# Two loads, one store and the first microseconds of a fused attention and feed-forward kernel, rearranged

## The chip, the cores and the metric

One Trainium2 chip, one core of it. The metric is the device time of one execution in microseconds (us). Before the change the median of three runs is 107.88 us (107.62 to 108.11). One further execution was profiled; it took 107.41 us, and the span that its profile covers is 105.6 us.

The engines are named as the profile names them: PE (matrix multiply, with PEld for its weight loads), DVE (vector), ACT (scalar), POOL (GpSimd) and SP (the queue that issues most DMAs).

## The reference, cut to what matters

```python
def phi(x):                                   # r = 8, so phi(x) has 64 features
    a = einsum('rd,bhsd->bhsr', S1, x); b = einsum('rd,bhsd->bhsr', S2, x)
    return einsum('bhsi,bhsj->bhsij', a, b).reshape(..., 64)
q_p, k_p = phi(q), phi(k)                     # batch 4, heads 4, sequence 1088, head size 32
kv  = einsum('bhsf,bhsd->bhfd', k_p, v);      z = sum(k_p, axis=2)
num = einsum('bhsf,bhfd->bhsd', q_p, kv);     den = einsum('bhsf,bhf->bhs', q_p, z) + 1e-6
x   = (num / den) -> 4352 tokens of 128       # heads side by side
h   = x @ w_in                                # 128 -> 2048
out = (h - tanh(h)) @ w_out                   # 2048 -> 128, float32
```

The kernel uses that `h @ w_out` is linear: it computes `x @ (w_in @ w_out)` once per token with a folded 128 x 128 matrix (kept as a high and a low bf16 half, `whi` and `wlo`), and subtracts `tanh(h) @ w_out`, for which the tanh is taken of `-h`.

## The kernel before, in words

The program is a list of operations. Each has an engine, an estimated cost, the cells that it reads and writes, and a function that issues its instructions. The order of the operations on every engine is written out as a table of numbers, `ORDER` (lines 37 to 76); each engine runs its list strictly in that order and waits on semaphores where an operand comes from another engine. A planner (`schedule`, lines 141 to 230) goes through the same list with estimated durations. It decides only one thing in the instructions: where PE gets dummy matmuls on a zero tile `wz` (the "fill", lines 187 to 201) while it would otherwise be idle before the first layer begins.

Loads are issued by SP. A load may not be issued before all but the last 2.4 MB asked for have landed (`gated`, line 419), so some loads wait in SP's queue, and everything behind them in the queue waits with them.

Batch 0 goes through a path of its own before the main phase. The keys are loaded and turned (L574), projected (L583), turned back (L591). POOL and DVE form the 64 key products of each token (`wk`, L630). PE multiplies them with the values `vx` (L643, `values_first`); ACT copies the sums (`kvs`, L649), PE folds the four strips (L652), and ACT copies the result twice, masked, into a block-diagonal `kvb` (L656). The queries run beside it: projection (L752), `qab` (L760), denominators (L779 to L788), products `qp` (L662), PE transposes (L677), ACT copies `qpB`, the numerators (L694), and the copy to `xT` (L700), which is what the first layer reads. ACT also casts parts of `w_in` to bf16 (L844), POOL the rest and all of `w_out` (L848); PE turns `w_in` (L858) and multiplies it with `w_out` to get the folded matrix (L870, "wfold").

The main phase has ten windows of tokens: 256, 256, seven of 512, 256. For every window PE does the first layer (L913), ACT the tanh (L917), PE the second layer with `w_out` as weights (L926) and the folded product (L898), all adding into one PSUM bank; DVE turns that bank into `osb` (L932), and four DMAs per window and batch store it (L939), with runs of 128 bytes. Batches 1 to 3 are attended to in between, on a separate path with its own lines.

The values of batch 0 are loaded by four DMAs (L480): each fills 32 partitions of `vx`, with four runs (heads) of 1152 or 896 bytes in each partition. `S1` and `S2` are loaded as `s_raw` with 8 rows each (L439).

Of the kernel before, what the change touches and what calls it, by code (L numbers as in the profile page):

```python
# [8 lines left out]
ALU = mybir.AluOpType  # L9
# [4 lines left out]
R = 8  # L14
# [16 lines left out]
COLD = 6800  # L31
CHUNK = 256
# [20 lines left out]
    ),  # L53
    "scalar": (
# [4 lines left out]
    ),  # L59
    "vector": (  # L60
# [5 lines left out]
    ),  # L66
    "gpsimd": (
        "24 16 2 3 4 19 5 25 6 20 7 17 18 79 80 81 110 106 22 23 107 21 109 108 111 150 152 241 242 247 251 363 365 364 370 374 "
        "506 508 507 517 513 "
    ),  # L70
    "sync": (
# [22 lines left out]
class Program:  # L94
# [46 lines left out]
    def schedule(self):  # L141
# [21 lines left out]
        while left:  # L163
# [20 lines left out]
            if e == "tensor":  # L184
                if filling and o in self.fill_stops:
                    filling = False
                if filling and fills_from in order["vector"]:
                    free[e] = max(free[e], fills_from.at + fills_from.cost + 200, 1050)
                    while True:
# [3 lines left out]
                        if free[e] + long + 60 > o.at:  # L193
                            break
# [149 lines left out]
def bass_polysketch_attn__then__act_tanh_shrink_kernel(nc, q, k, v, S1, S2, moe_w_in, moe_w_out, out):  # L344
# [26 lines left out]
    e4 = sb("e4", [4, 4, 4, 8])  # L371
    hmask = sb("hmask", [128, 2])
    pmask = sb("pmask", [128, 2])
    mask = sb("mask", [128, H, R])
# [31 lines left out]
    tt = sb("tt", [128, UNITS, UNIT], BF16)  # L406
    osb = [sb(f"osb{i}", [128, 512]) for i in range(2)]
# [38 lines left out]
    def load_rows(dst, src, name, b, cuts, prios, first=0):  # L446
        i = b % 2
        for x, (lo, hi) in enumerate(cuts):
            hi = min(hi, S)
            size = 512 * (hi - lo)  # L450
            o = P.op("sync", size / (340 if b else 290), lambda e, lo=lo, hi=hi: e.dma_start(
                out=dst[i][:, lo:hi], in_=src[b].rearrange("h (j c) d -> (h j) (c d)", j=32)[:, lo:hi]),
                w=cells(name + "raw", i, lo, hi), sem=f"{name}{i}{x + first}", prio=prios[x], name=f"load {name}{b}{x + first}",
                after=gated(size))
            o.lag = 1500 if b == 1 else 300
            asked.append((o, size))
# [18 lines left out]
    def load_v(b, prio):  # L475
        i = b % 2
        src = v[b].rearrange("h (j c) d -> j h c d", j=32)
        for g in range(4):
# [3 lines left out]
                in_=src[:, :, 9 * g:9 * g + n, :].rearrange("j h t d -> j h (t d)")), True, 190 if b == 0 else 240)  # L482
# [19 lines left out]
    def constants():  # L502
# [7 lines left out]
        P.op("gpsimd", 240, lambda e: e.memset(e4[:, :, :, :], 0.0), w=[("e4",)], prio=-999)  # L510
        P.op("gpsimd", 400, select(e4[:, :, :, :], [[0, 4], [-1, 4], [0, 8]], 0), r=[("e4",)], w=[("e4",)], prio=-999)
# [6 lines left out]
        P.op("vector", 110, lambda e: e.memset(pmask[:, :], 0.0), w=[("pmask",)], prio=-998)  # L518
        for h in range(2):
            P.op("vector", 110, lambda e, h=h: e.memset(pmask[64 * h:64 * h + 64, h:h + 1], 1.0),  # L520
                 w=[("pmask",)], prio=-998)
# [11 lines left out]
    def sketch():  # L533
        def put(e):
            for h in range(H):
                ins = e.matmul(ps[32 * h:32 * h + 32, 5, 0:32], s_raw[:, :],
                               ident[0:16, None, 0:16].to_broadcast([16, 2, 16]),
                               start=True, stop=True, tile_position=(0, 32 * h))
            return ins

        P.op("tensor", 100, put, r=[("s_raw",), ("ident",)], w=[bank[5]], prio=-3000, mode="32x32", name="psk", ni=16)
# [6 lines left out]
    def folding():  # L548
        P.op("tensor", 60, lambda e: e.matmul(
            ps[:, 6, 0:32], e4[:, :, :, :].rearrange("p a b c -> p (a b c)"), e4[:, 0, :, :].rearrange("p b c -> p (b c)"),  # L550
# [515 lines left out]
```

## Time and profile before

| what | value |
|---|---|
| median of three runs | 107.88 us |
| the profiled execution | 107.41 us, span 105.6 us |
| busy over the span | PE 97.0 us, ACT 78.5, DVE 60.4, POOL 35.9 |
| values of batch 0, issue of their last load to landing | 4.70 to 9.23 us |
| first multiplication with the values (L643) | 9.93 us |
| first matmul of the first layer (L913) | 16.25 us |
| folded product (L870) | 19.34 us |
| last turn into `osb` (L932), last store issued | 102.06 us, 102.96 us |

Times inside the profile count from the start of the span. A group line gives engine, line, operation and tiles, then busy time and the mean of one, then the idle time ahead and what ended it. A line of the timeline gives start, length, engine, line and operation. The chain follows the last instruction back through what released it.

### The profile page before, as it was taken

How to read it: one execution, taken by the hardware profiler on the slowest of the kernel's cores; microseconds unless marked ns; L12 is line 12 of the kernel's file. 1: busy time of each engine (PE TensorE's matmuls, PEld its weight loads, DVE VectorE, ACT ScalarE, POOL GpSimd, SP SyncE). 2: the span in 40 equal slices, each digit the busy share in tenths (PEclk: the TensorE clock that was granted, in tenths of full speed). 3: DMA queues.
4: the chain of work that ended last, by engine and by line, in shares of the span. 5: the costliest groups of instructions: out<-in, count | busy, mean ns of one | idle time of the engine just before them, and what ended most of it. 6: DMA issues, size and time to landing. Idle time of an engine off the chain costs nothing.

```text
span 105.6 us, 2945 instructions
## 1 busy us (share of the span) xinstructions
PE 97.0 (92%) x1243; PEld 50.2 (48%) x1254; DVE 60.4 (57%) x128; ACT 78.5 (74%) x107; POOL 35.9 (34%) x45
## 2 busy tenths in 40 slices
PE   6899899999999969989899999999999999999960
PEld 2557556774576433423644343544444434345540
DVE  2378966899899999198389546892550020200210
ACT  3340588746768836769899796989969999899930
POOL 5637058710946700884900059176000000000000
PEclk9999999999999999999999999999999999999998
DMA  2999999603841503799202300035013222015263
GB/s 46 288 218 346 321 313 243 239 20 72 261 120 19 151 20 77 189 228 253 73 0 33 51 6 0 6 53 87 0 22 50 46 43 44 0 31 91 36 94 55
DMA packets 26509, 11.21 MB, mean 106 GB/s; under 512 B 19072, under 2 KB 24320, under 8 KB 26496
## 3 DMA queue, kind: packets, MB, share of 16 engines
q1 hardware_dynamic: 25920, 10.95, 42.9%
q8 instruction: 10, 0.16, 0.6%
q10 hardware_dynamic: 576, 0.07, 0.4%
q14 instruction: 3, 0.02, 0.1%
HBM read 8.78 MB, written 2.23 MB: 104 GB/s over the span
## 4 chain that ended last, share of the span: by engine, by line
PE 58%; DMA 12%; DVE 10%; ACT 5%; SPq 4%; POOL 4%; issue 3%; POOLq 0%; DVEq 0%
PE ps L926 21%; PE ps L913 21%; DMA w_out_f<-in_moe_w_out_dram 5%; ACT tt L917 5%; PE ps L821 4%; DMA vx<-in_v_dram 4%; PE ps L898 4%; DMA out_dram<-osb 3%; DVE qpT L804 3%; POOL w_out L848 2%; DVE qp L798 2%; DVE osb L932 2%; SPq L480 2%; PE ps L752 1%; DVE qab L760 1%
## 5 line engine op out<-in xcount | busy, mean ns | idle before, releaser
L917 ACT ACTIVATE tt<-ps 128x1024 bf16<-128x1024 f32 (+1 forms) x70 | 66.9, 998 | 10.9 <-PE ps L913 10.2
L913 PE MATMUL ps<-xT,w_in 128*128 128x512 bf16 (+1 forms) x151 | 40.4, 346 | 1.3 <-issue 0.6
L926 PE MATMUL ps<-tt,w_out 128*128 128x512 bf16 (+1 forms) x158 | 39.7, 347 | 0.2 <-issue 0.2
L630 POOL TENSOR_TENSOR wk<-kab 128x768 f32<-128x768 f32 (+2 forms) x11 | 15.7, 1424 | 22.7 <-DVE kab L591 22.2
L913 PEld LDWEIGHTS ps<-xT,w_in 128*128 128x128 bf16 x160 | 14.0, 97 | 17.5 <-ACT tt L917 5.5
L926 PEld LDWEIGHTS ps<-tt,w_out 128*128 128x128 bf16 x160 | 15.3, 99 | 13.2 <-issue 1.3
L932 DVE STREAM_TRANSPOSE osb<-ps 128x512 f32<-128x512 f32 (+1 forms) x10 | 6.4, 636 | 24.1 <-PE ps L926 22.9
L798 POOL TENSOR_TENSOR qp<-qa,qab 128x768 f32<-128x768 f32 x6 | 11.2, 1867 | 7.3 <-DVE qa L788 7.1
L804 DVE STREAM_TRANSPOSE qpT<-qp 128x768 f32<-128x768 f32 x9 | 8.4, 961 | 4.1 <-POOL qp L798 4.0
L760 DVE STREAM_TRANSPOSE qab<-ps 128x576 f32<-128x576 f32 (+2 forms) x10 | 6.0, 638 | 2.5 <-PE ps L752 2.5
L740 DVE STREAM_TRANSPOSE qT<-qraw 128x576 f32<-128x576 f32 (+2 forms) x9 | 5.8, 653 | 0.0
L504 PE MATMUL ps<-wz 128*128 128x512 bf16 x9 | 4.6, 581 | 1.0 <-DVE hmask L514 1.0
L821 PE MATMUL ps<-qpT,kvw 32*32 32x288 f32 (+1 forms) x192 | 4.6, 398 | 0.8 <-DVE qpT L804 0.8
L570 DVE STREAM_TRANSPOSE kT<-kraw 128x576 f32<-128x576 f32 x6 | 4.4, 746 | 0.0
L831 ACT CAST xT<-ps 128x256 bf16<-128x256 f32 x6 | 2.1, 380 | 2.8 <-PE ps L821 2.8
L898 PE MATMUL ps<-xT,whi 128*128 128x512 bf16 (+1 forms) x10 | 3.5, 353 | 0.7 <-DVE osb L932 0.4
L798 DVE TENSOR_TENSOR qp<-qa,qab 128x768 f32<-128x768 f32 x3 | 4.0, 1346 | 0.1
L848 POOL CAST w_out<-w_out_f 128x512 bf16<-128x512 f32 x4 | 2.4, 611 | 4.5 <-DMA w_out_f<-in_moe_w_out_dram 4.1
L591 DVE STREAM_TRANSPOSE kab<-ps 128x576 f32<-128x576 f32 (+2 forms) x5 | 3.2, 656 | 1.1 <-PE ps L583 1.1
L821 PEld LDWEIGHTS ps<-qpT,kvw 32*32 32x32 f32 x192 | 2.5, 103 | 2.8 <-DVE qpT L804 1.3
L712 PEld LDWEIGHTS ps<-wk,vx 128*32 128x32 f32 x216 | 3.2, 110 | 1.2 <-issue 1.2
L712 PE MATMUL ps<-wk,vx 128*32 128x64 f32 x216 | 3.6, 220 | 0.0
(90 smaller groups left out, 90.1 us busy)
## 6 DMA issues: line engine op xcount, KB each, us to landing
vx<-in_v_dram SPq DMA_DIRECT2D x12, 144.0 KB, 3.6
qraw<-in_q_dram SPq DMA_DIRECT2D x4, 288.0 KB, 4.6
w_in_f<-in_moe_w_in_dram SPq DMA_DIRECT2D x4, 256.0 KB, 4.8
w_out_f<-in_moe_w_out_dram SPq DMA_DIRECT2D x4, 256.0 KB, 5.9
out_dram<-osb SPq DMA_DIRECT2D x16, 64.0 KB, 2.0
kraw<-in_k_dram SPq DMA_DIRECT2D x3, 288.0 KB, 4.2
kraw<-in_k_dram SPq DMA_DIRECT2D x3, 256.0 KB, 4.1
qraw<-in_q_dram SPq DMA_DIRECT2D x3, 256.0 KB, 3.1
```

Source lines behind the costliest of these rows:

```text
L630: P.op(eng, dve(cols) if eng == "vector" else pool2(cols), lambda e, t0=t0, t1=t1, ap=ap, m=m, ka0=ka0: e.tensor_tensor(out=wk[:, t0:t1, : ...
L712: ins = e.matmul(ps[32 * h:32 * h + 32, vb, 0:64], vx[i][:, h, t, :], wk[:, t, h, :, :], start=(t == 0), stop=(t == NT - 1), tile_position ...
L740: P.op("vector", dve(hi - lo), lambda e: e.transpose(out=qT[i][:, lo:hi], in_=qraw[i][:, lo:hi]), r=cells("qraw", i, lo, hi), w=cells("qT" ...
L760: P.op("vector", dve(2 * n), lambda e, h=h: e.transpose(out=qab[:, t0:t1, h:h + 2, :].rearrange("p t h x -> p h t x"), in_=ps[:, qb + h:qb ...
L798: P.op(eng, dve(cols) if eng == "vector" else pool2(cols), lambda e, p0=p0, p1=p1, w=w: e.tensor_tensor(out=qp[:, p0:p1, :, :, :].rearrang ...
L804: P.op("vector", dve(cols), lambda e, p0=p0, p1=p1: e.transpose(out=qpT[:, p0:p1, :, :, :].rearrange("p t h y j -> p (t h y j)"), in_=qp[: ...
L821: ins = e.matmul(ps[32 * h:32 * h + 32, nb[g], 0:32 * n], kvw[i][32 * g:32 * g + 32, y, 32 * h:32 * h + 32], qpT[32 * g:32 * g + 32, t0:t0 ...
L898: P.op("tensor", pe(n), lambda e, x=x: e.matmul(acc[:, 0:n], x[:, :], xT[:, f0:f0 + n], start=f0 > 0 and x is whi, stop=not f0 and x is wl ...
L913: P.op("tensor", pe(n), lambda e, jb=jb + y, y=y, hb=hb: e.matmul(hb[:, n * y:n * y + n], w_in[:, 128 * jb:128 * jb + 128], xT[:, f0:f0 + ...
L917: P.op("scalar", act(q * n), lambda e, un=un, hb=hb, q=q: e.activation(out=tt[:, un, 0:q * n], in_=hb[:, 0:q * n], func=AF.Tanh, scale=-1. ...
L926: P.op("tensor", pe(n), lambda e, jb=jb, un=un, y=y: e.matmul(acc[:, 0:n], w_out[:, jb, :], tt[:, un, n * y:n * y + n], start=(not f0 and ...
L932: P.op("vector", dve(n), lambda e: e.transpose(out=osb[u][:, 0:n], in_=acc[:, 0:n]), r=[ka], w=[("osb", u)], prio=slot0, name=f"osb{w}")
```

## The change

Four parts, and a new written-out order for all engines.

1. The dummies before 5 us may run up to 120 ns past the planned start of an operation that has just become ready; the others still have to end 60 ns ahead of it.
2. The sketch: `s2p` (L552) becomes four column tiles of the same PE pass as `psk` (L536). The matmul that made the head mask (L549) goes, with its `e4` constant; the mask is now made on DVE by four small reductions of the identity. `kvb` is cleared once on POOL and then written by two plain ACT copies of 64 partitions, instead of two masked copies of 128; `pmask` goes.
3. The values of batch 0: four loads of 96 partitions, one for each head, and one of 32 partitions for the rest. The two loads of the first 512 columns of the queries become one.
4. The last 256 tokens: their `tanh` tiles and `xT` are used as weights and `w_out`, `whi`, `wlo` as the moving operand, 128 tokens at a time, in banks 6 and 7. The result has tokens in partitions, so a DVE copy and an ACT copy take the place of the turn, and two DMAs with runs of 512 bytes, one on SP and one on ACT, that of the four with runs of 128 bytes.

```diff
-                        if free[e] + long + 60 > o.at:
+                        if free[e] + long > o.at + (120 if o.at < EARLY and o.at - o.ready < 1 else -60):
...
-        src = v[b].rearrange("h (j c) d -> j h c d", j=32)
-        for g in range(4):
+        src = v[b].rearrange("h (j c) d -> j h (c d)", j=32)
+        for x in range(0 if b else 4):
+            rows = src[:, x, 0:KG]
+            rows = bass.AP(tensor=rows.tensor, offset=rows.offset, ap=[[KG, 3], *rows.ap])
+            o = load("sync", 128 * 32 * 27, ("vx", i), f"v{i}", prio, lambda e, x=x, rows=rows: e.dma_start(
+                out=vx[i][0:96, x, :, :].rearrange("p t d -> p (t d)"), in_=rows), True, 300)
+            o.lag = 300
+        for g in range(0 if b else 3, 4):
...
+        for g in range(4):
+            P.op("vector", 110, lambda e, g=g: e.tensor_reduce(
+                out=mask[32 * g:32 * g + 32, :], in_=ident[32 * g:32 * g + 32, 32 * g:32 * g + 32].rearrange("p (h i) -> p h i", i=R),
+                axis=AX.X, op=ALU.add), r=[("ident",)], w=[("mask",)], prio=-989, name=f"mask{g}")
+        P.op("gpsimd", 240, lambda e: e.memset(kvb[:, :, :, :], 0.0), w=[("kvb", 0), ("kvb", 1)], prio=-976)
...
             for h in range(H):
+                ins = e.matmul(ps[32 * h:32 * h + 32, 6, 64:96], e16[:, :, :].rearrange("p a b -> p (a b)")[:, 32 * h:32 * h + 32],
+                               s_raw[:, :], start=True, stop=True, tile_position=(0, 32 * h))
...
-            scaled(kvb[:, :, y, :], ps[:, vb, 0:128].rearrange("p (x y d) -> p x y d", x=2, y=2)[:, :, y, :], pmask[:, y:y + 1], 64,
-                   [bank[vb], ("pmask",)], [("kvb", y)], T["kvb"], f"kvb{y}")
+            P.op("scalar", act(64), lambda e, y=y: e.copy(
+                kvb[64 * y:64 * y + 64, :, y, :], ps[64 * y:64 * y + 64, vb, 0:128].rearrange("p (x y d) -> p x y d", x=2, y=2)[:, :, y, :]),
+                r=[bank[vb]], w=[("kvb", y)], prio=T["kvb"], name=f"kvb{y}")
...
+                    for dst, _, at in halves:
+                        ins = e.matmul(dst, tt[:, un, n * y + at:n * y + at + 128], w_out[:, jb, :], start=False, stop=jb == NJB - 1)
...
+            for y, (eng, queue) in enumerate((("vector", "sync"), ("scalar", "scalar"))):
+                P.op(eng, act(128) if y else dve(128), lambda e, y=y: (e.copy if y else e.tensor_copy)(
+                    olast[:, y, :], halves[y][0]), r=[bank[6 + y]], w=[("olast", y)], prio=slot0, name=f"osb{w}")
+                c = (f0 - (B - 1) * S) // 32 + 4 * y
+                P.op(queue, 65536 / 250, lambda e, c=c, y=y: e.dma_start(
+                    out=ob[B - 1, :, c:c + 4, :].rearrange("j c e -> c j e"), in_=olast[:, y, :]),
+                    r=[("olast", y)], sem=f"outlast{y}", prio=slot0, name=f"out{w}")
...
-    load_rows(qraw, q, "q", 0, q_cuts(0)[:2], (-948, -947))
+    load_rows(qraw, q, "q", 0, ((0, 512),), (-948,))
```

The new order, in names. SP before: three key loads, two query loads, four value loads, `w_in` 0, 3, 1, 2, `w_out` 2 (which waits for the values), a query load, `w_out` 1, 0, 3. SP after: three key loads, values of head 0, the query load, values of heads 1, 2, 3 and the rest, a query load, `w_in` 1, 0, `w_out` 1 (which waits for the values), `w_in` 2, 3, `w_out` 0, 3, 2. ACT before, from the first sums on: `kvs`, cast of `w_in` 0, `kvb` twice, `qpB` twice, cast of `w_in` 1, the first `w_inT`. ACT after: casts of `w_in` 1 and 0, `kvs`, `kvb` twice, `qpB` twice, the first `w_inT`. POOL after casts `w_in` 3 and 2 ahead of all of `w_out`; before, it began with `w_out` 2. On PE the first part of the product with the values (L643) now stands ahead of the query projection (L752), and the folded product of the last window ahead of that of the window before it.

More of the change, by code (lines that the diff above doesn't have):

```diff
@@ L31 @@
 COLD = 6800
+EARLY = 5000
 CHUNK = 256
@@ L535, in put @@
             for h in range(H):
-                ins = e.matmul(ps[32 * h:32 * h + 32, 5, 0:32], s_raw[:, :],
-                               ident[0:16, None, 0:16].to_broadcast([16, 2, 16]),
-                               start=True, stop=True, tile_position=(0, 32 * h))
+                e.matmul(ps[32 * h:32 * h + 32, 5, 0:32], s_raw[:, :],
+                         ident[0:16, None, 0:16].to_broadcast([16, 2, 16]),
+                         start=True, stop=True, tile_position=(0, 32 * h))
+            for h in range(H):
+                ins = e.matmul(ps[32 * h:32 * h + 32, 6, 64:96], e16[:, :, :].rearrange("p a b -> p (a b)")[:, 32 * h:32 * h + 32],
+                               s_raw[:, :], start=True, stop=True, tile_position=(0, 32 * h))
             return ins
-        P.op("tensor", 100, put, r=[("s_raw",), ("ident",)], w=[bank[5]], prio=-3000, mode="32x32", name="psk", ni=16)
+        P.op("tensor", 170, put, r=[("s_raw",), ("ident",), ("e16",)], w=[bank[5], bank[6]], prio=-3000, mode="32x32", name="psk", ni=32)
         for h in range(2):
@@ L548, in folding @@
     def folding():
[L549 to L556 removed]
         for h in range(H):
[L558 removed]
+            scaled(s2blk[:, h, :], ps[:, 6, 64:96], mask[:, h:h + 1], 32, [bank[6], ("mask",)], [("s2blk", h)], -850, f"s2blk{h}")
     KCUT = ((0, 576), (576, NT * 128))
@@ L894, in layers, with both @@
         xs = [("x", b, c // 4, c % 4) for b, lo, m, _ in parts(f0, n) for c in range(lo // 32, (lo + m) // 32)]
+        last = f0 + n == NTOK
+        halves = [(ps[:, 6 + y, 0:128], f0 + 128 * y, 128 * y) for y in range(2)]
         def lin():
             for x, nm in ((whi, "whi"), (wlo, "wlo")):
-                P.op("tensor", pe(n), lambda e, x=x: e.matmul(
-                    acc[:, 0:n], x[:, :], xT[:, f0:f0 + n], start=f0 > 0 and x is whi, stop=not f0 and x is wlo),
-                    r=[(nm,)] + xs, w=[ka], prio=slot0 + LAG - 0.5, name=f"lin{w}")
+                if last:
+                    def both(e, x=x):
+                        for dst, f, _ in halves:
+                            ins = e.matmul(dst, xT[:, f:f + 128], x[:, :], start=x is whi, stop=False)
+                        return ins
+                    P.op("tensor", pe(n), both, r=[(nm,)] + xs, w=[bank[6], bank[7]], prio=slot0 + LAG - 0.5, name=f"lin{w}", ni=4)
+                else:
+                    P.op("tensor", pe(n), lambda e, x=x: e.matmul(
+                        acc[:, 0:n], x[:, :], xT[:, f0:f0 + n], start=f0 > 0 and x is whi, stop=not f0 and x is wlo),
+                        r=[(nm,)] + xs, w=[ka], prio=slot0 + LAG - 0.5, name=f"lin{w}")
         where = []
@@ L938, in layers @@
             for eb in range(4):
-                P.op("scalar" if last and eb % 2 else "sync", 128 * m / 250, lambda e, b=b, c=c, mc=mc, eb=eb, at=at: e.dma_start(
+                P.op("sync", 128 * m / 250, lambda e, b=b, c=c, mc=mc, eb=eb, at=at: e.dma_start(
                     out=ob[b, :, c:c + mc, 32 * eb:32 * eb + 32],
                     in_=osb[u][32 * eb:32 * eb + 32, at:at + 32 * mc].rearrange("p (c x) -> p c x", x=32)),
-                    r=[("osb", u)], sem=f"out{u}s" if last and eb % 2 else f"out{u}", prio=slot0, name=f"out{w}")
+                    r=[("osb", u)], sem=f"out{u}", prio=slot0, name=f"out{w}")
     windows = [(0, 256, (2, 2, 4, 4, 4)), (256, 256, (4, 4, 4, 4))]
```

47 lines of the change are left out of this document (20 added, 27 removed), and 52 rows, old and new, of the table ORDER.

## The prediction

> **What bounds the kernel now.** I first read the busy time by stretch: one before the first matmul of the first layer, one to the end of PE's work, and the tail.
>
> ```profile
> 0.00:16.20 16.20, 14.35 (x226) 8.38 (x227) 10.25 (x38) 7.50 (x23) 7.59 (x24) 1.00 0.91 256
> 16.20:102.00 85.80, 82.64 (x1021) 41.81 (x1029) 49.75 (x90) 71.03 (x84) 28.34 (x21) 1.00 0.35 79
> 102.00:105.60 3.60, 0.00 (x0) 0.00 (x0) 0.45 (x1) 0.00 (x0) 0.00 (x0) 0.88 0.48 73
> ```
>
> The second number after the stretch is PE's busy time: 82.64 of 85.80 us from 16.2 to 102. PE bounds the main phase (going through the starts of its bf16 matmuls I find only 4.9 us of gaps there, the largest 0.96). So only three things set the end: when the first layer begins (16.25), PE's work, and the 3.6 us behind it. Whatever moves that begin moves the end. So next the chain that ended last, then the timeline of what comes ahead of 16.25.
>
> ```profile
> 4.70 4.53 DMA vx<-in_v_dram
> 9.25 4.83 DMA w_out_f<-in_moe_w_out_dram
> ...
> 19.34 1.07 PE ps L870 x16
> ...
> 100.86 1.11 PE ps L926 x10
> 102.06 0.45 DVE osb L932
> ```
>
> ```profile
> 9.93 1.23 PE L643 MATMUL ps<-wk,vx 128*32 128x64 f32 x72
> 11.21 0.27 ACT L649 COPY kvs<-ps 128x128 f32<-128x128 f32 x1 [3.06 <-PE ps L643]
> 11.37 0.62 ACT L844 CAST w_in<-w_in_f 128x512 bf16<-128x512 f32 x1
> 13.43 0.44 PE L694 MATMUL ps<-qpB,kvb 128*64 128x128 f32 x4
> 15.86 0.27 ACT L700 CAST xT<-ps 128x128 bf16<-128x128 f32 x1
> 16.25 0.49 PE L913 MATMUL ps<-xT,w_in 128*128 128x256 bf16 x3
> 102.54 0.89 ACTq L939 DMA_DIRECT2D out_dram<-osb  x2
> ```
>
> The values land at 9.23 (4.70 + 4.53), PE takes them at 9.93, and from `kvs` (11.21) to the first layer it is 5.04 us of ACT and PE in turn. Last, the DMA issues.
>
> ```profile
> vx<-in_v_dram SPq DMA_DIRECT2D x12, 144.0 KB, 3.6
> w_in_f<-in_moe_w_in_dram SPq DMA_DIRECT2D x4, 256.0 KB, 4.8
> s_raw<-in_S_dram ACTq DMA_DIRECT2D x2, 1.0 KB
> ```
>
> The reader is to see that `s_raw` alone has no time to landing. In the trace every DMA with an outer count of 128 or 32 posts 16 updates on its semaphore; the two of `s_raw`, with 8 rows, post 18 together, that is 8 and one each. A DMA is thus shared out along its outermost count, and eight rows use eight of the sixteen engines.
>
> **The values over 96 partitions.** The new source begins with a count of 3 (`[KG, 3]`), the destination with 96. Sharing along both outermost counts leaves 3 engines. The trace shows 16 and 8, not 3, so the cost is bounded by the two ends.
>
> With 3 engines: each load has 96 runs of 1152 bytes, the four 384, so 128 on each of the three. The packet records give 51 ns for such a packet (median). 128 x 51 ns = 6.53 us. In the same three rings lie the query load (8 packets of 2048 bytes at 84 ns, 0.67) and the 32-partition load (8 at 41 ns, 0.33). The keys leave them free at about 4.1 (their last packets start between 3.9 and 4.8). 4.1 + 6.53 + 0.67 + 0.33 = 11.6; the last of these packets came 0.9 ahead of the landing before, most engines' 0.6, so the values land at about 12.3, 3.1 later than 9.23. I take this end, because it is the only reading in which the `s_raw` row and the new count obey the same thing.
>
> With 16 engines: 24 packets each at 51 ns, 1.2 us, and the landing comes at about 7.9, 1.3 earlier.
>
> [...]
>
> **What is queued behind it.** On the three rings wait the query load behind the values (8 x 93 ns) and `w_in` 1 and 0 (16 x 84 ns): 11.6 + 2.1 = 13.7, landing at 14.4. ACT now casts `w_in` 1 and 0 (0.62 each) ahead of `kvs`; these were behind it. So `kvs` begins at 14.4 + 0.62 = 15.0. PE has the values at 12.3 and needs 1.23 for the sums and 0.50 for the query projection (L752), which stands behind the first of them: 14.0, no later. From `kvs` to the first layer 5.04 become about 4.3: one cast (0.62) is gone from between and the `kvb` copies are 0.2 instead of 0.3 (L555 copies 128x32 in 0.18). First layer at 19.3: **+3.1**. The query chain (projection to numerators 3.9 us) arrives at 12.6 + 3.9 = 16.5, and with the ACT work behind it at 19 as well.
>
> SP issues `w_in` 2, 3 and `w_out` 0, 3, 2 only after `w_out` 1 has seen the values, so from 12.7 on; before, all of `w_in` was issued by 7.0. They land at 15.9 to 19.2. POOL casts `w_in` 3 and 2 by 17.9, ahead of PE's third turn (needed near 18.5), and ends `w_out` at 20.9. PE reaches the folded product at about 21, so it hides; without that cover each late cast costs 0.62. PE's gaps between 16.2 and 20 (0.6 us, half of it waiting for L870 and its casts) shrink: **-0.3**.
>
> **The sketch, the masks, the dummies.** `s2p` (0.63 at 5.04, ahead of L583 at 5.60) goes; four more tiles behind `psk` cost at most its 0.33. The key chain gains about 0.35. Four DVE reductions (0.19, row L610) for three memsets (0.06) lie in DVE's 2.23 us of waiting for the keys; POOL's identity comes at 2.5 instead of 1.84, and the masks end at 3.6 against the keys at 3.96. The clearing of `kvb` is 0.2 on POOL, early. Dummies cost 0.12 once at most. If they bring the full clock sooner, L583, L599 and L607 lose about half of their 1.21 + 0.53 + 0.58 (a 512-column dummy still takes 0.61 at 7.89 and 0.39 at 11.09): up to 0.7. All of that ends in a wait for the values: 0 here, a gain only if they land early. Merged query load: 0.
>
> **The last window.** Two matmuls of 128 columns, each with its own weights, for one of 256: L870 does sixteen in 0.93 start to start, 58 ns each, against 109 for one of L926's 256-column ones: 18 x (116 - 109) = **+0.13**. Its folded product no longer waits for `osb` of the window before: **-0.2** of the two gaps there (0.19 and 0.18). Then the store. Before, from PE's end 102.06 to the last landing at 104.60: 2.54. After: copy 0.29 (L874, 128x128 from PSUM), 0.05, issue to first packet 0.84 (99.57 to 100.41), the packets, and 0.17 to land. The outermost counts are 4 and 128, so by the same reading both DMAs share four engines: 2 x 32 packets of 512 bytes at 27 ns = 1.73. Sum 3.08, **+0.54**. On 16 engines the packets take 0.43: 1.78, -0.76.
>
> **The sum.** 3.1 - 0.3 + 0.13 - 0.2 + 0.54 = +3.3. Against the profiled execution's own time (107.41: span 105.6 and 1.8 around it) 110.7. The median of the runs is 0.47 higher; on its scale 107.88 + 3.3, so I say 111.1. The kvs chain is the least sure: 109.6 to 112.6 for this case.
>
> **The rivals.** (1) *Faster: the loads are spread over all engines.* [...] Then the values land at 7.9 and other things set `kvs`: the key products, which gain the 0.35, and the two casts, whose `w_in` lands near 10.1. First layer 0.7 earlier; the last window 0.13 - 0.2 - 0.76 = -0.83. 107.88 - 1.5 = 106.4. It decides from a landing before about 9. (2) *Slower still:* PE now stands idle from about 9.4 to 12.3, and the clock falls back. The trace shows no such fall ahead of 104.7, so its price is that of the cold rows: L599 takes 0.53 at 7.43 and 0.38 at 26.67, 1.4 times; on L643, L652 and L694 (1.23 + 0.49 + 0.44) that is +0.8: 111.9. (3) *It does nothing:* the late values meet slack that I don't see, or the loads are spread and the store is not (-0.7 + 0.47): 107.7.
>
> **Chances.** Forecast 0.60; (2) 0.12; (1) 0.23; (3) 0.05. Three runs lie within 0.25% of their median, so 0.5% is about what can be told from no change. Slower 0.72, same 0.05, faster 0.23. The range goes from 106.2, in the first rival, to 112.6.
>
> **What would show it.** Right: no time to landing for the 108 KB value loads, as for `s_raw`; L643 not before 12; `kvs` behind two casts at about 15; L913 at 19; the last packets 1.7 us long behind two issues on SP and ACT. Wrong: L643 before 9.9, which would say that the sharing does not follow the outermost count; or a late landing with L913 still near 16, which would say that ACT's order has slack.

## The result, and the profile after

The changed kernel takes **114.44 us** (median of four runs, 113.82 to 115.31), the kernel before, run beside it, 107.75 (106.87 to 108.11). The ratio is **1.064, 95% interval [1.054, 1.074]**: slower, as forecast, but by 6.7 us and not by 3.2, and outside the range, whose upper end was 112.6. The profiled execution took 114.75 us, with a span of 112.9. In the table of runs further on, executions more than 1.5% above the fastest of their kernel are left out of the ratios, but not of the medians.

The busy time by stretch of the changed kernel comes first: the same three stretches as before, namely to the first matmul of the first layer, to the end of PE's work, and the tail. The columns are the stretch, its length, and the busy time of PE, PEld, DVE, ACT and POOL, then the granted clock, the DMA share and GB/s.

```profile
0.00:22.60 22.60, 15.85 (x234) 9.49 (x235) 10.53 (x39) 7.26 (x22) 8.15 (x26) 0.77 0.67 194
22.60:108.20 85.60, 83.87 (x1050) 42.52 (x1047) 50.55 (x90) 70.78 (x84) 27.40 (x19) 1.00 0.36 76
108.20:112.90 4.70, 0.01 (x1) 0.00 (x0) 0.29 (x1) 0.27 (x1) 0.00 (x0) 0.91 0.37 69
```

The main phase is as long as it was (85.60 against 85.80). The first stretch grew from 16.2 to 22.6, the tail from 3.6 to 4.7. Next, the chain of work that ended last, from the first value load on and in its last pieces (start, length, what):

```profile
2.33 0.90 SPq L482
...
6.02 7.35 DMA vx<-in_v_dram
...
13.41 0.65 PE ps L645 x16
...
107.10 1.13 PE ps L943 x20
...
108.25 0.29 DVE olast L957
```

Behind SP's issues of the keys the chain comes to the value loads and stays on them until 13.37; before, it left them at 9.23. The timeline of the changed kernel says what follows them (start, busy time, engine, line, operation; in brackets the idle time before it and what ended it):

```profile
13.41 0.65 PE L645 MATMUL ps<-wk,vx 128*32 128x64 f32 x16 [4.24 <-DMA vx<-in_v_dram]
14.80 1.32 ACT L847 CAST w_in<-w_in_f 128x512 bf16<-128x512 f32 x2 [7.49 <-DMA w_in_f<-in_moe_w_in_dram]
15.21 1.72 PE L645 MATMUL ps<-wk,vx 128*32 128x64 f32 x56
16.99 0.27 ACT L651 COPY kvs<-ps 128x128 f32<-128x128 f32 x1 [0.87 <-PE ps L645]
20.01 1.36 POOL L847 CAST w_in<-w_in_f 128x512 bf16<-128x512 f32 x2 [10.46 <-DMA w_in_f<-in_moe_w_in_dram]
22.46 2.11 POOL L851 CAST w_out<-w_out_f 128x512 bf16<-128x512 f32 x3
22.61 0.60 PE L927 MATMUL ps<-xT,w_in 128*128 128x256 bf16 x4
25.12 1.06 PE L873 MATMUL ps<-w_out,w_inT 128*128 128x128 bf16 x16
```

PE stands idle for 4.24 us before the values come. The product with them (L645, L643 before) needs 1.72 us for its last 56 matmuls, so `kvs` starts at 16.99 instead of 11.21, 5.78 later. From `kvs` to the folded product (L873, L870 before) it is 8.13 us, and it was 8.13 before: the folded product, too, moved by 5.78. To the same place at about the same time comes a second chain, POOL's casts: the first of `w_in` waits for its transfer until 20.01, the last of `w_out` ends at 24.57.

I take the folded product as the mark for the end of the head: from its start to the first copy (or turn) of the last window it is 82.72 us before and 83.13 after. So the 7.3 us of span are **5.78 (head) + 0.41 (main phase) + 1.04 (first copy to last landing: 102.06 to 104.82 before, 108.25 to 112.05 after)**, and 0.07 behind the last landing.

The mark is not quite even. Of the second layer, four matmuls stand ahead of the folded product before, and one after; the two rows, before and after:

```profile
18.68 0.60 PE L926 MATMUL ps<-tt,w_out 128*128 128x256 bf16 x4
25.02 0.27 PE L948 MATMUL ps<-tt,w_out 128*128 128x256 bf16 x1
```

Three such matmuls, started 0.11 us apart, are 0.33 us. By equal work the head is thus about 6.1 us later, and the main phase longer by no more than 0.1. So it is in every kernel below that has the new order of PE (e1, e3 to e7, e10, e11). The first layer begins 6.36 later (22.61 against 16.25).

The clock was not the same either. The row of the granted clock in 40 slices, and a table of PE's work in windows of 3.41 us, the length of the first stretch on the clock's record (full, 6.21 to 9.62); the half clock behind it is three times as long (10.24):

```profile
PEclk9997555999999999999999999999999999999998
```

```profile
6.20:9.62 3.42, 1.76 (x34) 0.98 (x26) 2.52 (x9) 0.37 (x2) 2.77 (x3) 1.00 0.75 225
9.62:13.03 3.41, 0.00 (x0) 0.00 (x0) 0.45 (x2) 0.00 (x0) 0.00 (x0) 0.50 0.45 130
13.03:16.45 3.42, 3.04 (x99) 2.17 (x103) 1.17 (x5) 1.24 (x2) 0.00 (x0) 0.50 0.60 178
16.45:19.86 3.41, 3.41 (x33) 2.21 (x27) 2.30 (x10) 1.06 (x5) 0.00 (x0) 0.50 0.80 224
```

The record of the clock begins at 6.2 (9.2 before) with a full clock; the row shows 9 ahead of that as well, but there it was half: a dummy of 512 columns takes 0.61 us at 4.28 and 0.39 at 6.28, and before the change 0.61 at 7.89 and 0.39 at 11.09. The clock falls to half at 9.62 and comes back only at 19.86, so the values are multiplied at half clock. The DMA rows bear out the reading of the outermost counts:

```profile
vx<-in_v_dram SPq DMA_DIRECT2D x4, 108.0 KB
out_dram<-olast ACTq DMA_DIRECT2D x1, 64.0 KB
out_dram<-olast SPq DMA_DIRECT2D x1, 64.0 KB
```

None of the three has a time to landing, like `s_raw` before. The semaphore of the values had 96 updates from nine DMAs: five of 16 and four of 3 + 1. Each of the last two stores gave five, 4 + 1. So the value loads ran on **three** engines and the stores on **four**. The packets say the same: around 8 us, 31 of them with 51 ns each ran in every half microsecond, about three at a time, which is the work of three engines; the 256 of the two stores, 27 ns each, took 1.89 us (109.83 to 111.71), or 3.7 at a time. The one record over comes early: for ACT's store at 109.61, ahead of its first packet at 109.83. A count of 8, in a run below, gives 8 + 1.

### The profile page after: what moved, and what is told of

It reads as the page before. It is cut to its first block, busy times and chain, and to the rows that moved or that the text cites. A ratio compares the mean times of both kernels' runs of the same rounds, so it can differ in the third digit from the quotient of the medians.

```text
span 112.9 us, 3007 instructions
## 1 busy us (share of the span) xinstructions
PE 99.7 (88%) x1280; PEld 52.0 (46%) x1280; DVE 61.4 (54%) x129; ACT 78.3 (69%) x107; POOL 35.5 (31%) x44
## 2 busy tenths in 40 slices
DMA packets 25505, 11.21 MB, mean 99 GB/s; under 512 B 17940, under 2 KB 23188, under 8 KB 25492
## 4 chain that ended last, share of the span: by engine, by line
PE 57%; DVE 16%; DMA 10%; SPq 9%; issue 2%; ACT 1%
PE ps L948 17%; PE ps L927 16%; DMA vx<-in_v_dram 7%; PE ps L824 4%; DMA out_dram<-osb 4%; DVE qab L763 3%; PE ps L912 3%; SPq L482 3%; PE ps L755 3%; DVE qpT L807 2%; SPq L969 2%; DVE osb L964 2%; PE ps L697 2%; PE ps L645 2%; PE ps L680 2%
## 5 line engine op out<-in xcount | busy, mean ns | idle before, releaser
L927 PE MATMUL ps<-xT,w_in 128*128 128x512 bf16 (+1 forms) x160 | 42.4, 348 | 0.3
L948 PE MATMUL ps<-tt,w_out 128*128 128x512 bf16 (+1 forms) x144 | 38.6, 356 | 0.0
L948 PEld LDWEIGHTS ps<-tt,w_out 128*128 128x128 bf16 x144 | 13.9, 99 | 13.1 <-issue 1.8
L964 DVE STREAM_TRANSPOSE osb<-ps 128x512 f32<-128x512 f32 (+1 forms) x9 | 5.9, 651 | 20.6 <-PE ps L948 19.4
L847 ACT CAST w_in<-w_in_f 128x512 bf16<-128x512 f32 x2 | 1.2, 619 | 7.6 <-DMA w_in_f<-in_moe_w_in_dram 7.5
L645 PE MATMUL ps<-wk,vx 128*32 128x64 f32 x72 | 2.4, 314 | 4.2 <-DMA vx<-in_v_dram 4.2
L511 PE MATMUL ps<-wz 128*128 128x512 bf16 x11 | 5.2, 582 | 1.0 <-DVE hmask L519 1.0
L847 POOL CAST w_in<-w_in_f 128x512 bf16<-128x512 f32 x2 | 1.2, 614 | 10.6 <-DMA w_in_f<-in_moe_w_in_dram 10.5
L645 PEld LDWEIGHTS ps<-wk,vx 128*32 128x32 f32 x72 | 1.9, 169 | 4.5 <-DMA vx<-in_v_dram 4.3
```

The source lines that it names most:

```text
L645: ins = e.matmul(ps[32 * h:32 * h + 32, tb, 0:64], vx[0][:, h, t, :], wk[:, t, h, :, :], start=(t == tiled[0][0]), stop=(t == tiled[-1][1] ...
L927: P.op("tensor", pe(n), lambda e, jb=jb + y, y=y, hb=hb: e.matmul(hb[:, n * y:n * y + n], w_in[:, 128 * jb:128 * jb + 128], xT[:, f0:f0 + ...
L948: P.op("tensor", pe(n), lambda e, jb=jb, un=un, y=y: e.matmul(acc[:, 0:n], w_out[:, jb, :], tt[:, un, n * y:n * y + n], start=(not f0 and ...
L964: P.op("vector", dve(n), lambda e: e.transpose(out=osb[u][:, 0:n], in_=acc[:, 0:n]), r=[ka], w=[("osb", u)], prio=slot0, name=f"osb{w}")
```

## The experiments

One table for all. The labels of the expectations are shortened in it. "Values" is when SP's wait for them ended, "folded" the start of the folded product, both in the profiled execution; the ratio is to the kernel before, run beside each.

| run | values | `kvs` | folded | last landing | median us | ratio, 95% |
|---|---|---|---|---|---|---|
| before | 9.25 | 11.21 | 19.34 | 104.82 | 107.75 | |
| after | 13.39 | 16.99 | 25.12 | 112.05 | 114.44 | 1.064 [1.054, 1.074] |
| e1 loads undone | 8.62 | 12.09 | 19.94 | 107.00 | 109.56 | 1.018 [1.015, 1.022] |
| e2 loads alone | 13.99 | 16.23 | 24.43 | 109.99 | 112.43 | 1.045 [1.040, 1.049] |
| e3 wait filled | 13.74 | 16.17 | 26.25 | 114.15 | 115.67 | 1.072 [1.064, 1.080] |
| e4 no late dummies | 13.56 | 16.64 | 24.87 | 112.19 | 114.59 | 1.066 [1.059, 1.072] |
| e5 `w_in` ahead | 14.14 | 17.65 | 25.22 | 112.29 | 115.53 | 1.071 [1.067, 1.075] |
| e6 ahead and filled | 14.20 | 16.75 | 24.43 | 111.80 | 113.94 | 1.054 [1.050, 1.059] |
| e7 loads undone, `w_in` ahead | 8.91 | 12.40 | 19.32 | 106.23 | 109.21 | 1.013 [1.009, 1.016] |
| e8 tail alone | 9.28 | 11.72 | 19.93 | 106.00 | 108.75 | 1.008 [1.005, 1.012] |
| e9 tail on eight | 8.95 | 11.81 | 19.58 | 105.08 | 107.77 | 1.001 [0.998, 1.004] |
| e10 values alone | 12.69 | 20.32 | 28.33 | 115.18 | 118.25 | 1.101 [1.095, 1.107] |
| e11 no loads, eight | 8.79 | 12.58 | 19.54 | 105.53 | 108.22 | 1.006 [1.002, 1.009] |
| e12 values late on 16 | 13.21 | 15.62 | 22.92 | 108.92 | 111.43 | no interval |
| e13 loads alone, filled | 14.29 | 15.83 | 23.21 | 109.11 | 111.70 | 1.032 [1.026, 1.038] |
| e14 as e12 | 13.61 | 14.91 | 22.99 | 109.25 | 110.72 | 1.028 [1.023, 1.034] |

My first theory was that of the prediction: part three makes the loss, because the values come late on three engines. Three causes could sit inside that: the values' own lateness, the clock that falls while PE waits, and the loads of weights that stand behind the wait in SP's queue.

### Part three away, and part three alone

e1 is the changed kernel with the value loads of before (`load_v`) and this; e2 is the kernel before with the reverse.

```diff
-    load_rows(qraw, q, "q", 0, ((0, 512),), (-948,))
+    load_rows(qraw, q, "q", 0, q_cuts(0)[:2], (-948, -947))
```

> The changed kernel with the loads of part 3 alone put back (four value loads of 32 partitions, two query loads), all else and the new order kept. Theory A (the loss begins with the values on three engines, landing at 13.4 instead of 9.2, and everything else of it follows from that): landing back near 9, no fall of the clock, first layer between 15.3 and 16.3, and only the tail's loss of about 1.2 us left: 107.0 to 109.0 us. Theory B (the new order, with two casts ahead of the sums on ACT and loads behind a wait, costs by itself): first layer after 17.5, above 110.

> The kernel before with the new loads of part 3 alone, in its old order. Theory A: landing at about 13, first layer near 21 to 22.5, no loss in the tail: 112 to 114 us. Theory B: below 110, since the old order has no casts ahead of the sums and all four w_in loads go out ahead of the wait.

Measured: 109.56 without it, 112.43 with it alone. The second is inside its band, the first above it: part three costs about 4.7 us (112.43 against 107.71), and all the rest a further 1.9 (109.56 against 107.71). Part three is the main cause, but the rest costs far more than the +0.5 that the prediction's terms for it sum to.

### The clock and the late dummies, in the changed kernel

In e3 the planner is told that the values land 5 us later, so that dummies fill the wait; in e4 the dummies stop ahead of the query projection.

```diff
-            o.lag = 300
+            o.lag = 5300
...
-        P.fill_stops = {o for o in P.ops if o.eng == "tensor" and o in P.wrote.get(bank[FB], ())}
+        P.fill_stops = {o for o in P.ops if o.name == "qproj0.0"}
```

> The changed kernel, its plan told that the values land 5 us later, so that PE has some 20 dummies of 512 columns in the wait and other dummies behind it. The landing stays at 13.4. Theory A with the clock as its second step: granted clock 1.0 from 13.4 on, the 72 matmuls with the values in 1.2 us instead of 2.4, first layer 1.5 to 2.5 us earlier: 112.0 to 113.0. If the fall of the clock is beside the path (ACT's casts and w_in's landings set the first layer): 114.2 to 114.8.

> The changed kernel without the dummies behind the first product with the values (0.39, 0.29, 1.46 and 0.42 us of them run there at half clock, after the wait). Theory A with the dummies as its third step: kvs and the fold 1.4 us sooner, the first layer 0.8 to 1.5 earlier: 113.0 to 113.7. If ACT and w_in set the first layer: 114.2 to 114.8.

Neither is faster: 115.67, above both bands of its expectation, and 114.59, in the band of its second one. In e3 the clock stayed full and `kvs` came 0.8 earlier, at 16.17. It came no earlier than that because ACT's two casts of `w_in` held it: PE's sums had ended at 15.57, and `w_in` 0 had landed only at 15.62. The folded product came later than in the changed kernel, at 26.25. That number should not be used by itself: the profiled execution is the longest of the four (116.87 us, the others 114.81 to 116.31), and its `w_in` 3 landed at 21.54 instead of 19.96. Its list of waits shows whose turn it was:

```profile
POOL w_in L847 <- DMA w_in_f<-in_moe_w_in_dram: 12.3, 1, 12.3
...
PE ps L861 <- POOL w_in L847: 2.4, 1, 2.4
```

POOL waited 12.3 us for a `w_in` block, and PE then 2.4 us for POOL. In e4, too, the folded product waited for POOL, for 0.40 us. So I took as the next theory that the binding chain is the queue: `w_out` 1, which holds SP's wait for the values, then `w_in` 2 and 3 behind it, then POOL's casts. The four runs of the changed kernel itself show no order by clock either (mean clocks 0.951, 0.991, 0.959 and 1.0, times 114.75, 115.31, 114.14 and 113.82), which is weak evidence, since the record can miss a half clock at the start, as it does here ahead of 6.2.

### The queue freed, cold and warm

In the changed kernel's table 43 is `w_out` 1, and 39 and 40 are `w_in` 2 and 3. e5 moves it behind them (the lines are a piece of SP's table); e6 has this and the longer lag of e3, e7 this and the loads of e1.

```diff
-41 38 37 43 39 40 42 45 44
+41 38 37 39 40 43 42 45 44
```

> The kernel after, with one entry of SP's order moved: w_in 2 and 3 are issued ahead of w_out 1, which holds the wait for the values, as in the kernel before; the other three blocks of w_out stay behind it. Theory A (what is queued behind the wait ends last): w_in 3 lands at about 16.5 instead of 19.96, POOL's two casts of w_in end at about 18 instead of 21.37, the first layer begins at 21.4 to 21.8 as where the loads were changed alone (21.55), and the time is 113.0 to 113.9. Rival B (the late values and the half clock set the head by themselves, the queue lies beside them): the first layer stays within 0.3 us of 22.61 and the time at 114.1 to 114.9.

> As the run before it (w_in 2 and 3 ahead of the wait), and the stretch in which TensorE waits for the values is also filled with dummy products, so that the clock stays up. If the queue behind the wait was hiding the clock (theory A), the fill now pays: kvs at about 16.2 as in the earlier filled run, the first layer 4.3 us behind it at about 20.5, time 111.8 to 112.9. If the clock's fall is beside the path even so, the time is that of the run before it within 0.4 us.

> The kernel after with the value and query loads of before and with w_in 2 and 3 ahead of w_out 1 as well. The run with the loads alone undone had its first layer at 17.41, behind POOL's cast of a w_in that had landed at 15.07. Theory A: w_in 3 lands by 13.5, the first layer begins at 16.2 to 16.9, and the time is 108.4 to 109.2, what is left over the kernel before being the tail. Rival B (the dense early dummies or the casts ahead of kvs hold the head): 109.4 to 109.8.

The theory of the queue alone **fell**: e5 took 115.53, no gain. `w_in` 3 landed at 17.51 instead of 19.96, but it now ran beside the values; these landed 0.75 later (14.14), still at half clock, and `kvs` at 17.65. What was won on one chain was lost on the other. With the clock kept up as well, e6 took 113.94, 1.6 under e5 and 0.5 under the changed kernel, within the uncertainty of the latter, and between the two bands of its expectation. In e6 neither the clock nor `w_in` behind the wait is left, and the folded product still starts at 24.43, 5.1 after that of before (5.4 by equal work): most of the loss stays with the late values. As in e3, some of it is ACT's casts, which wait for `w_in` 0 (landed at 16.20): PE's sums end at 16.03, `kvs` begins at 16.75.

In e7, where the values are early, the same swap counts: the folded product at 19.32 against 19.94 in e1, 109.21 against 109.56, at the edge of theory A's band. So the new order of SP seems to cost some 0.4 to 0.6 when the values are early, and nothing that I can see when they are late; the intervals of the two ratios overlap by a hair (1.009 to 1.016 and 1.015 to 1.022).

### The tail

e8 is the kernel before with the code of the last window from after, and these ends of ACT's and SP's order:

```diff
-736 739 760 762
+736 739 760 761
...
-717 718 759 761
+717 718 759
```

> The kernel before with the last part alone: the last 256 tokens are the weights of the second layer, two copies, two stores. Theory A (the two stores go over four engines, and SP's one stands behind the stores of the window before): the last landing is 3.6 to 3.9 us behind TensorE's end instead of 2.54, the time 108.6 to 109.2. As the prediction priced it (0.13 - 0.2 + 0.54): 108.1 to 108.4. Rival (the tail was long only because of the order of after's last products): 107.5 to 107.9.

108.75 against 107.81: +0.94, theory A's band. (These expectations count 2.54 for the kernel before, from 102.06 to SP's last landing; ACT's was later, at 104.82, so 2.76 is right, and e8 has 3.65.) To see whether the four engines make it, the halves were cut another way: even and odd tokens, so that a half holds 16 rows of each of eight blocks and the store begins with a count of 8.

The same edit is made to e8 (this is e9) and to e7 (e11).

```diff
-        halves = [(ps[:, 6 + y, 0:128], f0 + 128 * y, 128 * y) for y in range(2)]
+        halves = [(ps[:, 6 + y, 0:128], f0 + y, y) for y in range(2)]
...
-                        ins = e.matmul(dst, tt[:, un, n * y + at:n * y + at + 128], w_out[:, jb, :], start=False, stop=jb == NJB - 1)
+                        ins = e.matmul(dst, tt[:, un, n * y + at:n * y + 256:2], w_out[:, jb, :], start=False, stop=jb == NJB - 1)
...
-                    out=ob[B - 1, :, c:c + 4, :].rearrange("j c e -> c j e"), in_=olast[:, y, :]),
+                    out=ob[B - 1, y:32:2, c:c + 8, :].rearrange("j c e -> c j e"), in_=olast[:, y, :]),
```

> The kernel before with the last part alone, as the run before, but the two halves of the last 256 tokens are the even and the odd ones instead of the first and the last 128, so that the stores' outermost count is 8 instead of 4. Theory A (the loss of the last part, 0.94 us, is the drain of both stores over the same four engines: some 64 packets of 512 bytes at 27 ns on each): eight engines drain in half of it, each store gives 9 semaphore updates, the last landing is 2.8 to 3.2 us behind TensorE's end instead of 3.7, and the time is 107.6 to 108.2. Rival (the loss is in the copies, in the longer issue of such stores, or in the split products): 108.5 to 109.1, with the last landing at 3.5 us or more behind TensorE's end.

> All of the change but its value and query loads, with w_in 2 and 3 ahead of w_out 1 and with the last tokens halved into even and odd: the run with w_in ahead (109.21) with the stores on eight engines. Theory A: 0.6 to 0.9 less, 108.3 to 108.6. If parts one and two cost nothing, what is left over before is this tail. Rival: no gain, 109.0 to 109.5.

e9 takes 107.77 against 107.73, in theory A's band: the loss is gone, and the semaphores of the two stores have nine updates each, 8 + 1. The ends of the two timelines, first e8, then e9:

```profile
102.35 0.29 DVE L955 COPY olast<-ps 128x128 f32<-128x128 f32 x1 [2.30 <-PE ps L941]
102.65 0.64 ACTq L958 DMA_DIRECT2D out_dram<-olast  x1
102.67 0.68 SPq L958 DMA_DIRECT2D out_dram<-olast  x1
```

```profile
102.14 0.29 DVE L955 COPY olast<-ps 128x128 f32<-128x128 f32 x1 [2.30 <-PE ps L941]
102.43 0.70 ACTq L958 DMA_DIRECT2D out_dram<-olast  x1
102.45 0.75 SPq L958 DMA_DIRECT2D out_dram<-olast  x1
```

Copies and issues are alike. The 256 packets of 512 bytes run from 103.93 to 105.67 in e8, 1.74 us, and from 103.77 to 104.75 in e9, 0.98, at 27 ns each in both. That is what 64 of them in turn on each of four engines take (1.73 us), and a little over 32 on each of eight (0.86): both stores use the same few engines, so here the second queue did not help. e11 takes 108.22, just under theory A's band, 1.0 under e7 (the ratios: 1.006 and 1.013). Against e9, which has neither parts one and two nor the new order, that leaves about 0.5 us for these, though the two intervals overlap. In the profiled executions it is in the head: `kvs` begins at 12.58, behind two casts, against 11.81, and the first layer at 17.02 against 16.47 (the folded products, at 19.54 and 19.58, differ by the three matmuls named above). The tails are alike, 2.96 and 2.95 us, although SP's last store is issued 0.28 behind ACT's in e11.

### What makes the values late

In e10, `w_out` 1 with the wait goes ahead of the query's second load and of all of `w_in`.

```diff
-41 38 37 43 39 40 42 45 44
+43 41 38 37 39 40 42 45 44
```

> The kernel after with w_out 1, and so SP's wait for the values, moved ahead of the query's second load and of w_in 1 and 0: nothing but keys, the query's first 512 columns and the values is on the queues until the values are there. If the other loads' packets slowed the values' three engines (theory A), they land at 11.5 to 12.6, near the 12.3 of the prediction, instead of 13.37; if the three engines alone set it (rival B), at 13.2 or later. The weights are issued some 5 us later in either case, so the time is 114 to 117 and no test of this.

With nothing else behind them the values landed at 12.69 instead of 13.39, between the two theories. From 5.5 on their packets kept to a median of 51 to 52 ns; in the changed kernel the medians by half microsecond are 66 to 84 ns from 8.5 to 11, when packets of other loads (2304 and 2048 bytes) ran beside them, and 51 again behind that. So about 0.7 us of the landing goes with the other loads (e3 and e4, with the same queue, land at 13.74 and 13.56), and 3.4 us over before is left with three engines and little company. The weights, all late now, made the time 118.25.

### Lateness without the three engines, and the clock by itself

e12 and e14 are one kernel: the kernel before, with the value loads (33 to 36 in its table, of which a piece is shown) behind those of `w_in`, still on 16 engines. e13 is e2 with the longer lag of e3.

```diff
-28 29 30 31 32 33 34 35 36 37 40 38 39 44 41
+28 29 30 31 32 37 40 38 39 33 34 35 36 44 41
```

> The kernel before with nothing of the change in it: only the four value loads, still over 16 engines, are moved behind the four w_in loads in SP's order, so that the values land late while all of w_in lands earlier than before. Theory A (the cost of part three is that the values come late, by whatever cause, and TensorE has nothing else to do): the values land at 12.2 to 13.5, the first layer begins 7 to 8 us behind that at 19.8 to 21.2, and the time is 110.9 to 112.6, close to the loads alone (112.43). Rival B (what costs is the crowding by the three-engine loads: w_in and w_out landing late, POOL's casts late): 107.7 to 109.5.

> The kernel before with part three alone, as in the earlier run (112.43), and the stretch in which TensorE waits for the values filled with dummies. In that kernel all of w_in is ahead of SP's wait, so that only the late values and the cold clock are left: there the 72 products with the values took 2.15 us instead of 1.23. Theory A (the clock's part of the loss is real where nothing else ends later): the products take 1.2, the folded product begins 0.8 to 1.2 earlier than 24.43, and the time is 111.3 to 111.9. Rival B (the clock is beside the path here too): 112.2 to 112.8.

> The kernel with the value loads on 16 engines behind those of w_in, once more, since one of its four times (109.68) lies apart from the others (111.4 to 111.5). If the lateness of the values alone makes most of the loss of part three (theory A): the larger share of the times at 111 to 111.6. If the crowding of the queues makes it (rival B): the larger share at 109.5 to 110, with w_out 3 landing well ahead of 21.7, behind which the folded product stood.

e12 has nothing of the change. Its four times, 109.68 and three of 111.38 to 111.50, lie too far apart to be priced, but are all above before. Repeated, it took 110.72 (110.27 to 111.80, ratio 1.028): not the two groups that I had expected, and again all above before (106.86 to 109.11). In the repeat's timeline the values land at 13.61 and the folded product begins at 22.99, where it waits for a late `w_out` as well:

```profile
13.63 1.21 PE L643 MATMUL ps<-wk,vx 128*32 128x64 f32 x72
14.91 0.27 ACT L649 COPY kvs<-ps 128x128 f32<-128x128 f32 x1 [6.88 <-PE ps L643]
22.32 0.62 POOL L848 CAST w_out<-w_out_f 128x512 bf16<-128x512 f32 x1 [1.40 <-DMA w_out_f<-in_moe_w_out_dram]
22.99 1.07 PE L870 MATMUL ps<-w_out,w_inT 128*128 128x128 bf16 x16 [0.62 <-POOL w_out L848]
```

So late values, without part three's loads, cost about 3 us (1.028), most of what part three costs; the late `w_out` behind SP's wait is included in that. e13 shows the clock's share where `w_in` is not behind the wait: 111.70 (1.032), in theory A's band, against 112.43 (1.045) without the dummies. In e2 the clock does not fall in the wait, it has not come up: a dummy of 512 columns takes 0.61 us at 8.69 and still 0.61 at 16.10. What e13 prices is thus a half clock in this place, whatever made it. The 72 products went from 2.15 us to 1.21, and the folded product from 24.43 to 23.21:

```profile
14.55 1.21 PE L650 MATMUL ps<-wk,vx 128*32 128x64 f32 x72
15.83 0.27 ACT L656 COPY kvs<-ps 128x128 f32<-128x128 f32 x1 [7.80 <-PE ps L650]
23.21 1.06 PE L877 MATMUL ps<-w_out,w_inT 128*128 128x128 bf16 x16
```

That is 0.7 us by the medians, or about 1.3% by the two ratios, whose intervals nearly touch. Three engines with a full clock (1.032 [1.026, 1.038]) and sixteen engines with late values (1.028 [1.023, 1.034]) cannot be told apart.

**The sum.** Each against before: part three about +4.7, of it, by the ratios, some 3 to 3.5 for the lateness, and 0.7 to 1.3 for the clock; the tail +0.9; parts one and two with the new order +0.5; the place of `w_in` 2 and 3 +0.4. That is 6.5 of the measured 6.7. The agreement should not be leaned on. The last two terms are differences of ratios whose intervals overlap. And e3, e5 and e6 show that the parts overlap, since in the changed kernel two chains reach the folded product within about half a microsecond of each other (POOL's casts end at 24.57, the product starts at 25.12). What stays open is how the clock and the queue divide their share in the changed kernel itself. No version beat the kernel before; e9 equals it.

## Why the prediction was right or wrong

Direction and mechanism were right; the size was not. By the prediction's steps:

- **"What bounds the kernel now"**: held. The main phase kept its length, and the end moved with the head and the tail.
- **"The values land at about 12.3"**: the three engines were right, the same three for all four loads (their packets ran three at a time), the time 1.1 short (13.37). Of that, about 0.7 goes with the loads beside them, which e10 took away; the prediction gave the neighbours their packets but kept 51 ns for the values' own, which were 66 to 84 beside other loads. In the kernel before, too, packets of 1152 bytes took 51 ns only at times: the medians are 51 from 4.5 to 5.5, 99 from there to 6.5, then 73 and 83 to 7.5. The rest stays open. It is not the longer issue of such a load on SP (0.70 to 0.90 us against 0.43): all four had been issued by 5.98, and the second one's packets began only at 6.88. The first one's 96 packets took from 3.97 to 6.5, where 32 at 51 ns on each engine are 1.63 us, with single packets of up to 0.74 us; why, no run shows.
- **"So `kvs` begins at 15.0"**: it began at 16.99, and not behind the two casts, which ended at 16.12, but behind PE's sums. Of the 2.0 us, 1.1 is the landing and 0.9 the sums at half clock. In e3, at full clock, it was behind the casts as forecast. The second rival, the clock falling back while PE stands idle, had a chance of 0.12 and a price of 0.8. Its mechanism came true (half clock from 9.62 to 19.86), and e13 prices a half clock there at 0.7 to 1.3 where nothing else ends later. It should have been in the forecast and not beside it. The clock fell when PE had been idle for 0.44 us, at the end of a window of 3.41 us in which it had been busy for half (1.76 us), so that the forecast idle stretch of 2.9 us, longer than that, was no reason to expect a full clock.
- **"From `kvs` to the first layer 5.04 become about 4.3"**: did not happen; it was 5.62. In its way stood matmuls at half clock, three dummies (1.46 us from 16.86) between the sums and the folding of the strips, and the late `w_in`; how the loss divides among them was not tried alone.
- **"-0.3"**: came about, at 0.25. From the first layer to the folded product it was 2.51 us instead of 3.09. Of the 0.58 between, 0.33 are the three matmuls that now stand behind it, and 0.25 is the gap that closed (before, the product waited there for POOL's cast of `w_out`).
- **"They land at 15.9 to 19.2 ... so it hides"**: `w_in` 2 and 3 and the rest of `w_out` landed at 18.21 to 22.84, and POOL ended `w_out` at 24.57, not at 20.9. The cover was thinner than the prediction had it, as e4 shows, and e3 with the reserve made above: once the values' chain gets shorter, POOL's ends last. The predicted way out, a free queue, gave nothing (e5).
- **The head in one number**: first layer +3.1 forecast, +6.36 measured; with the -0.3, +2.8 forecast and +6.1 measured. The 3.3 us between are 1.1 (landing at 13.37 for 12.3), 0.9 (sums at half clock) and 1.3 (5.62 for 4.3 behind `kvs`). **This is the step that failed**: the mechanism was the right one, its size came out at half.
- **Sketch, masks, dummies at 0**: with the new order they cost about 0.5 us (e11 against e9). The gains named for them are there, the key projection starting 0.47 earlier (5.14 for 5.61) and, in this execution, the clock 3 us sooner, and are lost in the wait for the values, as forecast. That the dummies bring the clock sooner is not shown: with the same ones it came at 10.05 in e1 and at 8.58 in e11, and at 3.64 in e7.
- **The last window, "+0.13", "-0.2" and "+0.54"**: the tail was +1.04. The drain of four engines was right (1.73 forecast, 1.89 measured, 1.74 in e8), and e9 shows that it is the cause. Issue to first packet was 1.29 us and not 0.84, SP's store was issued 0.22 behind ACT's because four stores of the window before stood ahead of it, and the landing of before had been read 0.22 too early (104.60 is SP's; ACT's came at 104.82). For the matmuls the two small terms fit: in e8 and e9, with the last window alone changed, the main phase is 0.30 and 0.17 shorter (82.42 and 82.55 us) where -0.07 was forecast.
- **Rival 1**, all engines and 106.4, is refuted by the 3 + 1 updates and by the landing at 13.37. **Rival 3**, nothing, by the result.

## What to carry to other kernels

Read the outermost counts of both sides of a DMA before anything else: here a count of 3 or 4 on one side left 13 or 12 of 16 engines out (3 + 1 and 4 + 1 updates), a second queue did not bring them back (e8: 256 packets in 1.74 us), and recutting which rows go together (even and odd tokens for the first and last 128) doubled the count at no cost that the time shows (e9: 107.77 against 107.73). When an early load comes late, do not only shift the chain behind it: price a half clock while the matrix engine waits (0.7 to 1.3 us here, e13), and the other loads that run beside it (0.7 us here, e10). And when two chains arrive together, freeing one of them may show nothing (e5: 115.53, for 114.44 in the changed kernel); take both away before calling either of them harmless.

## What the runs showed of the hardware

- In the changed kernel the clock fell at 9.62, when PE had been idle for only 0.44 us; in the 3.41 us before, it had been busy for 1.76. It then stayed at half for 10.24 us, through a window in which PE was busy for 3.04 of 3.42 us, mostly with small float32 matmuls, and rose after one of 3.41. Busy time alone does not tell these apart: in e7 it rose at 3.64, after a window with 2.65 us of PE, all of it dummies (the 17 dummies of 512 columns of e7 took 455 ns in the mean, the 11 of the changed kernel 582).
- The clock's row can be wrong at the start, where the record has not begun: the kernel with the loads alone (e2, record from 17.94) shows a full clock throughout its head, while its 72 products took 2.15 us against 1.21 to 1.23 in before, e13 and e14.
- In the head, a load over 96 partitions with a count of 3 took SP 0.70 to 0.90 us to issue, one over 32 partitions 0.43 to 0.47.
